# DeltaNet + MoE on one core: the first chunk's matmuls in float32r parts, weight loads that wait for the conversion, and a background inversion that waits for the softplus

## The chip, the cores and the metric

One core of a Trainium2 chip runs the whole program. The metric is the device time of one execution in microseconds (us). The kernel before took 718.76 us, the median of three runs (718.11 to 719.0). One more execution was profiled: it took 716.53 us, of which the trace shows a span of 714.8 us.

The engines named below are PE (the matrix engine, with its weight loads shown as PEld), DVE (vector), ACT (activation), POOL and SP, which issues the transfers.

## The reference

Two stages follow each other. The first is a recurrent attention over 768 steps for 4 x 8 heads of width 48, the second a two-layer MLP with a softplus between, over 3072 tokens (384 -> 2048 -> 384):

```python
for t in range(S):
    kt, vt, bt = (k_n[:, :, t], v[:, :, t], beta[:, :, t, None])
    y[:, :, t] = np.einsum('bhd,bhde->bhe', q[:, :, t], state)
    v_old = np.einsum('bhde,bhd->bhe', state, kt)
    state = state + bt[:, :, :, None] * np.einsum('bhd,bhe->bhde', kt, vt - v_old)
...
h = x @ w_in
g = np.maximum(h, 0.0) + np.log1p(np.exp(-np.abs(h)))
return (g @ w_out).astype(np.float32)
```

`k_n` is `k` divided by its norm. The weights of the MLP come as 64-bit floats, and the kernel turns them into 32-bit ones itself.

## The kernel before, in words

**Chunks.** The 768 steps are cut into 12 chunks of 64 (`NS`, `C`). A chunk's attention needs the inverse of a triangular matrix for every head; the inversion is done for two chunks at once (`invert(u, ...)`, chunks 2u and 2u+1), on DVE, a column at a time (lines 220 and 226). For u = 0 and 1 only the 16-wide diagonal blocks are inverted so, and `join` puts them together with products on PE (lines 243 and 250). `finish` turns the inverse into the tile `tt` with two transposes on DVE (lines 232 and 233). After it come `cross_a`, `arrange`, `cross_b` (lines 260 to 284), `k_state`, `p_half`, `u_all`, `y_all` (line 342 makes the chunk's output, lines 347 to 352 copy it into the tile `x`, line 360 moves a quarter of it by DMA), and `state`.

**MLP.** A chunk has 256 tokens. The hidden width is cut into 16 blocks f of 128, taken in 8 pairs. A pair is: the first product into `ph` (line 462), three passes on ACT (lines 466 to 468), the softplus and its split on DVE (lines 470, 472, 473), and, one pair later, the second product into `po` (line 445). All chunks but the first use three products of float32r parts in place of one product in float32 (high x high, high x low, low x high: `TERMS`). The first chunk uses plain float32 for both products (`HF`, and line 476 in place of 470 to 473).

**Weights.** A generator `weights()` (the `conversion`) turns block f from 64-bit to 32-bit: one pass on ACT (line 381), four on DVE (lines 393, 396, 400, 403), one copy on ACT (line 406). It begins with the first chunk. In the second chunk `split(f)` copies the block out (line 413), rounds it to its high part (line 415) and subtracts for the low part on DVE (line 416), all in the same buffer `w{f}`. A load of block f + 4 is put into the program when block f is converted; ahead of it line 391 writes one column of the new buffer.

**Order.** The order of PE, DVE, ACT and POOL is laid out when the program is built: the code is written by hand in the order of `attention()`, `moe()` and the calls of `fill(n)`, which advance the conversion by n steps, and a planner then places each engine's instructions by its own estimates. An instruction without anything to wait for can move far ahead: the eight one-column writes of line 391 for blocks 8 to 15 stand at the very start of DVE's order. `attend`, `target()` (`RATE`, `LEAD`, `FIRST`) decide how far the attention runs ahead of the MLP, and `invert_some` advances the background inversion by two columns for each half pair of the MLP.

The tile `ex` has three buffers and serves the conversion, the split and the output.

Of the kernel before, what the change touches and what calls it, by code (L numbers as in the profile page):

```python
# [7 lines left out]
F32 = mybir.dt.float32  # L8
# [27 lines left out]
def deltanet_moe(ctx, tc, kT, qT, kN, kI, vN, beta, wts, out):  # L36
# [36 lines left out]
    W, HF, ST, OFF, TT, LTD, LDS, NN, NV, X = {}, {}, {}, {}, {}, {}, {}, {}, {}, {}  # L73
# [112 lines left out]
    def invert(u, cT, ncT):  # L186
# [49 lines left out]
    def join(s):  # L236

        tt = TT[s // 2][:, s % 2 * NP:(s % 2 + 1) * NP, :]
        w1 = two.tile([P, NP, QB], F32, name="gl")
# [15 lines left out]
    def cross_a(s):  # L255
# [7 lines left out]
        if s < 2:  # L263
# [12 lines left out]
    def cross_b(s):  # L276
# [6 lines left out]
        for h in range(2):  # L283
            copies[s < 2 and h](tt[lo[h], :, HB:], pm[lo[h]])
# [27 lines left out]
    def u_all(s):  # L312
# [4 lines left out]
        for e in range(2):  # L317
            for ab in range(2):
                copies[s < 2 and ab](be[tk[ab], ab, e, :, C:], pus[e][tk[ab]])  # L319

    def state(s):
        for g in range(2):
# [6 lines left out]
            for ab in range(2):  # L329
                copies[s < 1 and ab](bv[dr[ab], ab, 8 * g:8 * g + 8, C:], pd[dr[ab]])  # L330

    def y_all(s):

        n, ty = (1, F32) if s == 0 else (2, F32R)
        x = X[s] = one.tile([P, n, NK, B, C], ty, name=f"x{s % 3}")
        x4 = one.tile([P, n, B, C], ty, name="x4")
        for g in range(2):
# [8 lines left out]
            copy = copies[s == 0 and g]  # L346
# [23 lines left out]
    def weights():  # L370
# [13 lines left out]
        ex = magnitude(0)  # L384
        yield
        for f in range(NF):
            hw, lw = words(f)
            if f + AHEAD < NF:

                ST[f + AHEAD] = one.tile([P, 4 * DM], I32, name=f"w{f + AHEAD}")  # L390
                nc.vector.memset(ST[f + AHEAD][:, 0:1], 0)
# [5 lines left out]
                                    op1=ALU.bitwise_and)  # L397
            after = magnitude(f + 1) if f + 1 < NF else None
            yield
# [5 lines left out]
            HF[f] = one.tile([P, 2 * DM], F32, name=f"w{f}")  # L405
            nc.scalar.copy(HF[f], ex.bitcast(F32))
            done[0], ex = f + 1, after
            yield

    def split(f):  # L410

        hf = two.tile([P, 2 * DM], F32, name="ex", bufs=3)
        nc.scalar.copy(hf, HF[f])
        w = W[f] = one.tile([P, 2, 2 * DM], F32R, name=f"w{f}")
        nc.scalar.copy(w[:, 0], hf)
        nc.vector.tensor_tensor(w[:, 1], hf, w[:, 0], op=ALU.subtract)


    def moe():


        n = B * C
        late = None
        for s in range(NS):
            parts = 2 if s else 1
            xr = [[X[s][:, i, k].rearrange("p b t -> p (b t)") for k in range(NK)]
                  for i in range(parts)]
            terms1 = TERMS if s else ((0, 0),)

            def weight(f, a, c, n, s=s):  # L430
                return W[f][:, a, c:c + n] if s else HF[f][:, c:c + n]

            po = ps_o.tile([P, 2, 512], F32, name="po")

            def outp(f0, g, po=po, s=s, weight=weight):

                k = 2 * len(g) - 1
                terms = [(f, h, i) for f in range(f0, f0 + 2) for h in range(2) for i in range(k)]
# [3 lines left out]
                for f, h, i in terms:  # L442
                    a, b = ((0, 0), (1, 0), (0, 1))[i]
                    end = f == NF - 1 and i == k - 1
                    nc.tensor.matmul(po[:, h, 0:DM], g[b][:, f - f0, h * P:(h + 1) * P],  # L445
                                     weight(f, a, DM, DM), start=(f == 0 and i == 0), stop=end)
# [4 lines left out]
            for f0 in range(0, NF, 2):  # L451
                while done[0] < f0 + 2:
                    next(conversion)
                if s == 1:
                    for f in range(0 if f0 == 0 else f0 + 2, min(f0 + 4, NF)):
                        split(f)
                ph = ps_h.tile([P, 2, n], F32, name="ph")
                for f in range(f0, f0 + 2):
                    c = 0
                    for k in range(NK):  # L460
                        for a, b in terms1:
                            nc.tensor.matmul(ph[:, f - f0], weight(f, a, k * P, P), xr[b][k],  # L462
                                             start=(c == 0), stop=(c == len(terms1) * NK - 1))
# [5 lines left out]
                if s:  # L469
                    nc.vector.scalar_tensor_tensor(a, ph, 0.0, a, op0=ALU.max, op1=ALU.add)  # L470
                    g = [two.tile([P, 2, n], F32R, name=name) for name in ("gh", "gl")]
                    nc.vector.tensor_copy(g[0], a)  # L472
# [298 lines left out]
```

## Time and profile before

| what | value |
|---|---|
| median of three runs | 718.76 us |
| the profiled execution | 716.53 us, span 714.8 us |
| PE busy | 631.6 us (88%) |
| DVE busy | 457.5 us (64%) |
| ACT busy | 369.4 us (52%) |
| mean clock granted to PE | 0.956 |
| transfers | 44.80 MB, most of it in the first quarter |

Busy time is summed over the span, and the stages differ: up to about 200 us the attention of chunks 0 to 2, the conversion of the weights and the first MLP chunk share the engines, and after that a period of about 51 us a chunk repeats. In the rows below, "L462" is line 462 of the kernel, "idle" the time the engine stood still before an instruction, and "issue" a wait for which the profile shows no releaser.

### The profile page before, as it was taken

Reading aid. Unit: us, or ns where it says so; the run is one execution under the profiler, and the core shown is the slowest. Engines: PE = TensorE matmul, PEld = TensorE weight load, DVE = VectorE, ACT = ScalarE, POOL = GpSimd, SP = SyncE. Lnnn points to the kernel's source line nnn. Section 1 sums busy time; section 2 is a strip of 40 time slices with the busy share of each in tenths; the row PEclk is TensorE's granted clock in tenths of the full one; section 3 lists DMA queues with packets and bytes.
Section 4 is the critical chain, followed back from the end, with each engine's and each line's share of the span. In section 5 each row is a group of like instructions: output and inputs, shape, how many; then the busy total and the mean of one; then the engine's idle time right before and its main releaser. Section 6 shows DMA issues by size and latency. Waiting matters only on the chain.

```text
span 714.8 us, 24068 instructions
## 1 busy us (share of the span) xinstructions
PE 631.6 (88%) x10736; PEld 583.5 (82%) x10736; DVE 457.5 (64%) x976; ACT 369.4 (52%) x681; POOL 30.1 (4%) x56
## 2 busy tenths in 40 slices
PE   4448877858998899998899997999998999999997
PEld 3447655537898898997899997899997999999997
DVE  5834799866746993466993467984449964454443
ACT  3222377819844356464357465365663556544443
POOL 3100100000000000000001000001000000000000
PEclk9999899979797999998999999899999999999999
DMA  9974250000022021032031130120310300201000
GB/s 224 367 280 120 68 137 10 0 2 25 4 71 78 23 68 46 13 88 61 23 86 38 48 100 27 45 57 25 73 31 24 79 2 25 59 3 33 1 23 22
DMA packets 35095, 44.80 MB, mean 63 GB/s; under 512 B 21776, under 2 KB 27184, under 8 KB 34992
## 3 DMA queue, kind: packets, MB, share of 16 engines
q1 hardware_dynamic: 34992, 43.27, 21.2%
q8 instruction: 84, 1.38, 0.8%
q14 instruction: 19, 0.16, 0.1%
HBM read 36.27 MB, written 4.72 MB: 57 GB/s over the span
## 4 chain that ended last, share of the span: by engine, by line
PE 65%; DVE 21%; issue 6%; ACT 6%; DMA 2%; SPq 0%; POOL 0%; DVEq 0%; ACTq 0%; POOLq 0%
PE po L445 24%; PE ph L462 23%; DVE work L220 3%; PE pa L342 3%; DVE Z L226 3%; PE pa L301 2%; PE pa L260 2%; PE pa L327 2%; PE pa L281 2%; DVE ltq L199 1%; DVE a L470 1%; DVE big L308 1%; DVE ex L403 1%; PE pa L315 1%; PE pa L131 1%
## 5 line engine op out<-in xcount | busy, mean ns | idle before, releaser
L462 PE MATMUL ph<-x,w 128*128 128x256 f32 x1680 | 247.4, 299 | 16.6 <-DVE a L470 9.0
L462 PEld LDWEIGHTS ph<-x,w 128*128 128x128 f32 x1680 | 228.3, 197 | 26.0 <-DVE a L470 9.7
L445 PE MATMUL po<-w,gh 128*128 128x384 f32 x768 | 214.9, 367 | 8.1 <-DVE gh L472 4.2
L466 ACT ACTIVATE a<-ph 128x512 f32<-128x512 f32 x96 | 57.4, 598 | 214.3 <-PE ph L462 203.4
L470 DVE SCALAR_TENSOR_TENSOR a<-ph,a 128x512 f32<-128x512 f32 x88 | 60.6, 689 | 155.5 <-ACT a L468 155.1
L445 PEld LDWEIGHTS po<-w,gh 128*128 128x128 f32 x768 | 139.3, 195 | 20.3 <-issue 6.6
L445 PE MATMUL po<-w,gl 128*128 128x384 f32 x352 | 121.2, 344 | 0.2 <-DVE gl L473 0.2
L445 PEld LDWEIGHTS po<-w,gl 128*128 128x128 f32 x352 | 67.8, 193 | 1.1 <-DVE gl L473 0.7
L473 DVE TENSOR_TENSOR gl<-a,gh 128x512 fp32r<-128x512 f32 x88 | 60.7, 690 | 3.8 <-PE po L445 0.7
L467 ACT ACTIVATE a<-a 128x512 f32<-128x512 f32 x96 | 60.7, 633 | 2.8
L468 ACT ACTIVATE a<-a 128x512 f32<-128x512 f32 x96 | 60.7, 632 | 2.4
L220 DVE TENSOR_TENSOR work<-Z,ltq 128x84 f32<-128x84 f32 (+14 forms) x148 | 44.0, 304 | 3.3 <-ACT gh L213 0.6
L226 DVE TENSOR_TENSOR Z<-Z,work 128x84 f32<-128x84 f32 (+14 forms) x148 | 44.1, 305 | 2.9
L472 DVE CAST gh<-a 128x512 fp32r<-128x512 f32 x88 | 38.0, 432 | 7.8 <-PE po L445 4.4
L342 PEld LDWEIGHTS pa<-big 128*64 128x64 f32 x768 | 26.0, 145 | 7.6 <-ACT big L319 2.6
L342 PE MATMUL pa<-big 128*64 128x64 f32 x768 | 28.8, 232 | 3.4 <-ACT big L319 2.1
L308 DVE TENSOR_TENSOR big<-pa,maskP 64x512 f32<-64x512 f32 x44 | 30.2, 686 | 1.6 <-PE pa L301 1.0
L301 PE MATMUL pa<-big,kt 48*64 48x64 f32 x704 | 27.7, 231 | 1.6 <-ACT off L118 0.9
L274 POOL MEMSET tt<- 32x512 f32 x24 | 13.2, 550 | 368.1 <-PE pa L260 203.2
L319 ACT COPY big<-pa 64x384 f32<-64x384 f32 x44 | 20.6, 472 | 13.1 <-PE pa L315 12.5
L301 PEld LDWEIGHTS pa<-big,kt 48*64 48x64 f32 x704 | 25.1, 145 | 2.0 <-ACT off L118 1.1
L330 ACT COPY big<-pa 48x384 f32<-48x384 f32 x42 | 19.9, 474 | 8.9 <-PE pa L327 8.3
(104 smaller groups left out, 648.4 us busy)
## 6 DMA issues: line engine op xcount, KB each, us to landing
w<-wts SPq DMA_DIRECT2D x16, 768.0 KB, 11.7
kt<-kT SPq DMA_DIRECT2D x24, 192.0 KB, 4.2
big<-qT SPq DMA_DIRECT2D x24, 192.0 KB, 4.1
nv<-vN SPq DMA_DIRECT2D x12, 384.0 KB, 4.1
ki<-kI SPq DMA_DIRECT2D x24, 192.0 KB, 3.5
out<-ex SPq DMA_DIRECT2D x24, 192.0 KB, 1.9
ka<-kN SPq DMA_DIRECT2D x8, 384.0 KB, 3.2
x<-x SPq DMA_DIRECT2D x66, 32.0 KB, 2.1
```

The source lines that it names most:

```text
L220: nc.vector.tensor_tensor(tmp[:, a:a + r, 0:j], Z[:, a + j + 1:a + n, a + j:a + j + 1].to_broadcast([P, r, j]), lq[:, a + j:a + j + 1, a:a ...
L226: nc.vector.tensor_tensor(z, z, tmp[:, a:a + r, 0:j], op=ALU.add)
L301: nc.tensor.matmul(pt[tk[ab], i, :], kts[s % 3][dr[ab], 8 * g + i, :], bv[dr[ab], ab, 8 * g + i, 0:C], start=True, stop=True)
L342: nc.tensor.matmul(py[tk[ab], i, :], big[:, at + C:at + 2 * C], big[:, at:at + C], start=True, stop=True)
L445: nc.tensor.matmul(po[:, h, 0:DM], g[b][:, f - f0, h * P:(h + 1) * P], weight(f, a, DM, DM), start=(f == 0 and i == 0), stop=end)
L462: nc.tensor.matmul(ph[:, f - f0], weight(f, a, k * P, P), xr[b][k], start=(c == 0), stop=(c == len(terms1) * NK - 1))
L466: nc.scalar.activation(a, ph, AF.Abs)
L467: nc.scalar.activation(a, a, AF.Exp, scale=-1.0)
L468: nc.scalar.activation(a, a, AF.Ln, bias=1.0)
L470: nc.vector.scalar_tensor_tensor(a, ph, 0.0, a, op0=ALU.max, op1=ALU.add)
L472: nc.vector.tensor_copy(g[0], a)
L473: nc.vector.tensor_tensor(g[1], a, g[0], op=ALU.subtract)
```

## The change

All twelve chunks now use the float32r parts. `HF` and `split` are gone: the conversion's last copy on ACT rounds straight to the high part (`W[f][:, 0]`), and the low part is subtracted on DVE one block later, from the same `ex` buffer, which is held until then. `y_all` makes both parts of `x` for chunk 0 as well, and several copies of chunks 0 and 1 that were shared between ACT and DVE are on ACT alone (`s < 2` became `s < 1`, or ACT only).

The one column of a new weight buffer is now copied from the block being converted (`ex[:, 0:1]`), so that the load of block f + 4 waits until block f has come that far. The calls of `fill` before the MLP starts advance the conversion by 25 steps in place of 16, and a block has five steps in place of four.

`invert_some` is wrapped in `tc.issue_after(softplus...)`: the planner may not put a column of the inversion ahead of the last softplus written before it. The small tile `ld` of the joins and its partner move from the buffers `gh` and `gl` into a spare `x` tile.

```diff
@@ invert
+            spare = one.tile([P, 2, NP, HB + QB], F32, name=f"x{u + 1}")
             for j in range(2):
-                ld = LDS[2 * u + j] = two.tile([P, NP, HB], F32, name="gh")
+                ld = LDS[2 * u + j] = spare[:, j, :, 0:HB]
+                LDS[2 * u + j, 1] = spare[:, j, :, HB:]
@@ y_all
-        n, ty = (1, F32) if s == 0 else (2, F32R)
+        n, ty = 2, F32R
...
-            copy = copies[s == 0 and g]
+            copy = nc.scalar.copy
@@ weights
-                nc.vector.memset(ST[f + AHEAD][:, 0:1], 0)
+                nc.vector.tensor_copy(ST[f + AHEAD][:, 0:1], ex[:, 0:1])
                 load_weights(f + AHEAD)
...
+            if f > 0:
+                nc.vector.tensor_tensor(W[f - 1][:, 1], last.bitcast(F32), W[f - 1][:, 0],
+                                        op=ALU.subtract)
+                done[0] = f
+                yield
...
-            HF[f] = one.tile([P, 2 * DM], F32, name=f"w{f}")
-            nc.scalar.copy(HF[f], ex.bitcast(F32))
-            done[0], ex = f + 1, after
+            W[f] = one.tile([P, 2, 2 * DM], F32R, name=f"w{f}")
+            nc.scalar.copy(W[f][:, 0], ex.bitcast(F32))
+            last, ex = ex, after
-    def split(f):
-        hf = two.tile([P, 2 * DM], F32, name="ex", bufs=3)
-        nc.scalar.copy(hf, HF[f])
-        w = W[f] = one.tile([P, 2, 2 * DM], F32R, name=f"w{f}")
-        nc.scalar.copy(w[:, 0], hf)
-        nc.vector.tensor_tensor(w[:, 1], hf, w[:, 0], op=ALU.subtract)
@@ moe
-                if s:
-                    nc.vector.scalar_tensor_tensor(a, ph, 0.0, a, op0=ALU.max, op1=ALU.add)
-                    g = [two.tile([P, 2, n], F32R, name=name) for name in ("gh", "gl")]
-                    nc.vector.tensor_copy(g[0], a)
-                    nc.vector.tensor_tensor(g[1], a, g[0], op=ALU.subtract)
-                else:
-                    g = [two.tile([P, 2, n], F32, name="gh")]
-                    nc.vector.scalar_tensor_tensor(g[0], ph, 0.0, a, op0=ALU.max, op1=ALU.add)
+                nc.vector.scalar_tensor_tensor(a, ph, 0.0, a, op0=ALU.max, op1=ALU.add)
+                g = [two.tile([P, 2, n], F32R, name=name) for name in ("gh", "gl")]
+                nc.vector.tensor_copy(g[0], a)
+                softplus[0] = nc.vector.tensor_tensor(g[1], a, g[0], op=ALU.subtract)
@@ invert_some
-        for _ in range(n):
-            if background and next(background[0], 0) == 0:
-                background.pop()
+        with tc.issue_after(softplus[0].ins):
+            for _ in range(n):
+                if background and next(background[0], 0) == 0:
+                    background.pop()
```

**Where the order moves.** A row is a line of the code, the operation, the tile written and the tiles read, their shape, and how often it comes in a row; a number behind a tile's name tells buffers apart.

The first place is SP's queue, after the loads of the first three `kt` tiles. Before:

```order
L368 DMA w_112<-wts 128x1536
L368 DMA w_114<-wts 128x1536
L368 DMA w_1413<-wts 128x1536
L368 DMA w_1424<-wts 128x1536
L368 DMA w_1525<-wts 128x1536
L368 DMA w_1536<-wts 128x1536
L368 DMA w_1564<-wts 128x1536
L368 DMA w_1575<-wts 128x1536
L368 DMA w_1610<-wts 128x1536
L368 DMA w_1621<-wts 128x1536
L95 DMA ka<-kN 128x768
L79 DMA kt_74<-kT 48x1024 x2
```

The same place in the change:

```order
L370 DMA w_112<-wts 128x1536
L370 DMA w_114<-wts 128x1536
L95 DMA ka<-kN 128x768
L79 DMA kt_74<-kT 48x1024 x2
L370 DMA w_631<-wts 128x1536
L370 DMA w_749<-wts 128x1536
L91 DMA nv<-vN 128x768
L370 DMA w_835<-wts 128x1536
L83 DMA big<-qT 48x16x64 x2
```

Eight weight loads that stood in a row (blocks 8 to 15) are gone from there; `ka` and `kt` come right behind blocks 2 and 3, and the further weight loads are spread behind them.

The second place is DVE at the end of the conversion. `ex` with `w` are passes of the conversion, line 416 the subtraction of a low part, `a`, `gh` and `gl` the softplus, `Z` and `work` the inversion for chunks 2 and 3. Before:

```order
L400 SCALAR_TENSOR_TENSOR ex<-w_1621,ex 128x768
L403 SCALAR_TENSOR_TENSOR ex<-w_1621,ex 128x768
L416 TENSOR_TENSOR w_1769<-ex,w_1769 128x768
L416 TENSOR_TENSOR w_1774<-ex,w_1774 128x768
L220 TENSOR_TENSOR work<-Z,ltq 128x14 x2
L226 TENSOR_TENSOR Z<-Z,work 128x14 x2
L220 TENSOR_TENSOR work<-Z,ltq 128x2x13 x2
```

In the change:

```order
L407 SCALAR_TENSOR_TENSOR ex<-w_1739,ex 128x768
L461 SCALAR_TENSOR_TENSOR a<-ph,a 128x512
L229 TENSOR_TENSOR Z<-Z,work 128x14 x2
L410 SCALAR_TENSOR_TENSOR ex<-w_1739,ex 128x768
L463 CAST gh<-a 128x512
L223 TENSOR_TENSOR work<-Z,ltq 128x2x13 x2
L464 TENSOR_TENSOR gl<-a,gh 128x512
L229 TENSOR_TENSOR Z<-Z,work 128x2x13 x2
L416 TENSOR_TENSOR w_1899<-ex,w_1899 128x768
L223 TENSOR_TENSOR work<-Z,ltq 128x3x12 x2
```

Before, the inversion's columns begin when the conversion is over and fourteen of the sixteen subtractions are still to come; now the last subtraction stands among the first columns, and the softplus has three instructions a pair in this stretch.

The third place is PE, just ahead of the first `join` of chunk 2 (line 243, now 246), which waits for the inversion. `x_832` and `x_844` are the input of chunk 0, `x_1303` and `x_1338` that of chunk 1. Before:

```order
L462 MATMUL ph<-x_832,w_1725 128x256 x3
L462 MATMUL ph<-x_832,w_1731 128x256 x3
L243 MATMUL pa<-tt,gh 32x16 x64
L445 MATMUL po<-w_1676,gh 128x384 x2
L445 MATMUL po<-w_1684,gh 128x384 x2
L462 MATMUL ph<-x_1303,w_1769 128x256 x9
L462 MATMUL ph<-x_1303,w_1774 128x256 x9
L445 MATMUL po<-w_1725,gh 128x384
```

In the change:

```order
L440 MATMUL po<-w_1892,gh 128x384 x2
L440 MATMUL po<-w_1892,gl 128x384
L440 MATMUL po<-w_1899,gh 128x384 x2
L440 MATMUL po<-w_1899,gl 128x384
L454 MATMUL ph<-x_1338,w_1602 128x256 x9
L454 MATMUL ph<-x_1338,w_1614 128x256 x9
L246 MATMUL pa<-tt,x_1783 32x16 x64
L440 MATMUL po<-w_708,gh 128x384 x2
```

Before, two second products of chunk 0 and all of chunk 1 stand behind the `join`; now chunk 0 is complete ahead of it, and so are the first products of four pairs of chunk 1.

More of the change, by code (lines that the diff above doesn't have):

```diff
@@ L238, in join @@
         tt = TT[s // 2][:, s % 2 * NP:(s % 2 + 1) * NP, :]
-        w1 = two.tile([P, NP, QB], F32, name="gl")
+        w1 = LDS[s, 1]
         pw = ps_a.tile([P, NP, QB], F32, name="pa")
@@ L283, in cross_b @@
         for h in range(2):
-            copies[s < 2 and h](tt[lo[h], :, HB:], pm[lo[h]])
+            copies[s < 1 and h](tt[lo[h], :, HB:], pm[lo[h]])
     def k_state(s):
@@ L318, in u_all @@
             for ab in range(2):
-                copies[s < 2 and ab](be[tk[ab], ab, e, :, C:], pus[e][tk[ab]])
+                copies[s < 1 and ab](be[tk[ab], ab, e, :, C:], pus[e][tk[ab]])
     def state(s):
@@ L329, in state @@
             for ab in range(2):
-                copies[s < 1 and ab](bv[dr[ab], ab, 8 * g:8 * g + 8, C:], pd[dr[ab]])
+                nc.scalar.copy(bv[dr[ab], ab, 8 * g:8 * g + 8, C:], pd[dr[ab]])
     def y_all(s):
-        n, ty = (1, F32) if s == 0 else (2, F32R)
+        n, ty = 2, F32R
         x = X[s] = one.tile([P, n, NK, B, C], ty, name=f"x{s % 3}")
@@ L382, in magnitude @@
             return ex
-        ex = magnitude(0)
+        ex, last = magnitude(0), None
         yield
@@ L424, in moe, with outp @@
         for s in range(NS):
-            parts = 2 if s else 1
             xr = [[X[s][:, i, k].rearrange("p b t -> p (b t)") for k in range(NK)]
[L427 to L431, printed above, removed]
+                  for i in range(2)]
             po = ps_o.tile([P, 2, 512], F32, name="po")
-            def outp(f0, g, po=po, s=s, weight=weight):
-                k = 2 * len(g) - 1
-                terms = [(f, h, i) for f in range(f0, f0 + 2) for h in range(2) for i in range(k)]
+            def outp(f0, g, po=po, s=s):
+                terms = [(f, h, i) for f in range(f0, f0 + 2) for h in range(2) for i in range(3)]
                 if f0 + 2 == NF:
@@ L443, in outp @@
                     a, b = ((0, 0), (1, 0), (0, 1))[i]
-                    end = f == NF - 1 and i == k - 1
+                    end = f == NF - 1 and i == 2
                     nc.tensor.matmul(po[:, h, 0:DM], g[b][:, f - f0, h * P:(h + 1) * P],
-                                     weight(f, a, DM, DM), start=(f == 0 and i == 0), stop=end)
+                                     W[f][:, a, DM:], start=(f == 0 and i == 0), stop=end)
                     if end:
@@ L460, in moe @@
                     for k in range(NK):
-                        for a, b in terms1:
-                            nc.tensor.matmul(ph[:, f - f0], weight(f, a, k * P, P), xr[b][k],
-                                             start=(c == 0), stop=(c == len(terms1) * NK - 1))
+                        for a, b in TERMS:
+                            nc.tensor.matmul(ph[:, f - f0], W[f][:, a, k * P:(k + 1) * P], xr[b][k],
+                                             start=(c == 0), stop=(c == 3 * NK - 1))
                             c += 1
@@ L630, in deltanet_moe @@
             mask_p(g, pts[g])
+        fill(2)
         run(jn)
         scale_v(0)
+        fill(2)
         cross_a(0)
```

24 lines of the change are left out of this document (13 added, 11 removed).

## Prediction

> **What bounds the kernel now.** First the page: the slices of the engines, and the chain that ended last.
>
> ```profile
> PE   4448877858998899998899997999998999999997
> DVE  5834799866746993466993467984449964454443
> DMA  9974250000022021032031130120310300201000
> PE 65%; DVE 21%; issue 6%; ACT 6%; DMA 2%; SPq 0%; POOL 0%; DVEq 0%; ACTq 0%; POOLq 0%
> ```
>
> A slice is a fortieth of the span, 17.9 us. PE is nearly full from the tenth slice on, so a gain there has to come out of its few idle stretches. The first nine slices look different: PE at 4 to 8, DVE at 9 around 90 to 125 us, the transfers at 9 in the first two. The busy times of stretches say it closer (columns: length, then busy us of PE, PEld, DVE, ACT, POOL, granted clock, share of the transfer engines, GB/s).
>
> ```profile
> 35.00:40.00 5.00, 1.38 (x83) 1.16 (x75) 0.00 (x0) 0.37 (x1) 0.00 (x0) 1.00 1.02 414
> 65.00:70.00 5.00, 4.29 (x157) 3.88 (x154) 2.17 (x4) 0.77 (x2) 0.00 (x0) 1.00 0.33 93
> 68.00:142.00 74.00, 60.02 (x759) 43.11 (x759) 64.03 (x120) 49.11 (x80) 3.55 (x6) 0.93 0.20 57
> 150.90:229.15 78.25, 71.51 (x1685) 64.80 (x1685) 42.40 (x68) 50.15 (x92) 3.51 (x5) 0.85 0.15 41
> 229.15:654.00 424.85, 408.10 (x6534) 387.86 (x6533) 281.62 (x597) 219.48 (x418) 12.40 (x19) 0.97 0.17 45
> ```
>
> Three regimes. At 35 to 40 us no engine works and the transfers run full. From 68 to 142 us DVE sets the pace (64.0 of 74.0 us). From 229.15, where PE starts the first product of chunk 2, PE is busy 408 of 425 us. I follow one landmark through the change, the start of chunk 2's first product ("M"), and treat what lies behind M apart.
>
> **The first stretch: held weight loads.** The chain of waits from 30 to 68 us (start, length, what):
>
> ```profile
> 30.76 3.44 issue
> ...
> 36.84 3.43 issue
> ...
> 43.32 3.14 issue
> ...
> 54.38 0.83 ACT w L406
> ...
> 63.29 0.94 issue
> ...
> 67.40 0.71 issue
> ```
>
> PE stops three times in the middle of a group of equal small products, for 10.0 us in all, while the transfers run full; at 63 and 67 us, with about a third of that load (the row of 65 to 70), the same stops are 0.9 and 0.7 us. I read them as PE's instructions arriving late behind the weight loads, ten of which SP issues in a row from 18 us. In the new order eight of the ten are gone from there. What is left ahead of 30 us is 8.4 MB (four blocks of 0.77, and the inputs); the trace moved some 8 MB by then. So the queue is empty at about 31 us and all three stops should shrink. Bounds: to nothing (10.0 gained), or to the longest stop seen without load, 2.04 us each (3.9 gained):
>
> ```profile
> 178.13 0.73 PE L243 MATMUL pa<-tt,gh 32*32 32x16 f32 x40 [2.04 <-issue]
> ```
>
> I take 1.0 each, nearest to the two rows at 63 and 67: 7.0 us. Against it stand additions on the same chain. ACT now rounds block 0 (0.83, row at 54.38) ahead of the copy that `cross_a` needs, and must wait for DVE's last pass before: 1.2 us. Chunk 0's `x` gets its low part on DVE, for two halves where it copied one before: 0.8 us; a conversion pass in front of them: 0.5 us. ACT also squares `ka` ahead of the first join's copy; `ka` now lands with the queue's end at about 30 us, before ACT reaches it at 33, so I cost it at nothing (each us later is a us on the chain). A held load makes SP wait for DVE's one-column copy; behind that of block 6 stand chunk 1's `q` and chunk 0's `x` transfers, but DVE makes this copy eight instructions before the last part of `x`, which those transfers need anyway. Net: the `x` transfers start 4.5 us earlier (between 1.4 and 7.5).
>
> **The second stretch: DVE.** Before, it runs from the last copy of chunk 0's `x` (61.0 us) to the end of the transpose that the first join of chunk 2 waits for (150.8 us), 89.8 us:
>
> ```profile
> 60.68 0.28 DVE L348 COPY x<-pa 128x128 f32<-128x128 f32 x1
> ...
> 97.60 0.56 DVE L393 TENSOR_SCALAR ex<-ex 128x768 f32<-128x768 f32 x1
> 98.07 0.95 DVE L400 SCALAR_TENSOR_TENSOR ex<-w,ex 128x768 int32<-128x768 int32 x1
> 98.94 0.95 DVE L403 SCALAR_TENSOR_TENSOR ex<-w,ex 128x768 int32<-128x768 int32 x1
> ...
> 148.86 1.90 DVE L232 STREAM_TRANSPOSE tt<-Z 128x1024 f32<-128x1024 f32 x1
> ```
>
> The starts are closer than the lengths: a short pass (lines 393, 396) costs about 0.5 us of DVE's time, a long one (400, 403) 0.87. So four passes are 2.75 us, and the subtraction (long, like line 400) 0.87. The softplus by its groups, less the same 0.08:
>
> ```profile
> L476 DVE SCALAR_TENSOR_TENSOR gh<-ph,a 128x512 f32<-128x512 f32 x8 | 5.5, 692 | 10.4 <-ACT a L468 5.2 <-PE po L445 4.8 <-PE pa L243 0.4
> L470 DVE SCALAR_TENSOR_TENSOR a<-ph,a 128x512 f32<-128x512 f32 x88 | 60.6, 689 | 155.5 <-ACT a L468 155.1
> L472 DVE CAST gh<-a 128x512 fp32r<-128x512 f32 x88 | 38.0, 432 | 7.8 <-PE po L445 4.4 <-PE pa L243 0.5
> L473 DVE TENSOR_TENSOR gl<-a,gh 128x512 fp32r<-128x512 f32 x88 | 60.7, 690 | 3.8 <-PE po L445 0.7
> L416 DVE TENSOR_TENSOR w<-ex,w 128x768 fp32r<-128x768 f32 x16 | 15.2, 953 | 7.6 <-ACT w L415 7.6
> L319 DVE COPY big<-pa 64x384 f32<-64x384 f32 x4 | 2.1, 557 | 1.4 <-ACT big L319 1.3
> ```
>
> A pair is 0.6 us in chunk 0 now, and 0.61 + 0.35 + 0.61 = 1.57 with parts. Counted over the same stretch of the two orders:
>
> - passes: 14 blocks and two passes before, 13 blocks and one after (a block more is done ahead of it): 40.2 to 36.6, -3.6
> - subtractions: 4 before, 14 after: +8.7
> - softplus: 6 pairs at 0.6, against 9 at 1.57 and one first instruction: 3.6 to 14.7, +11.1
> - six copies that go to ACT (0.56 by the last row above, two of them a third larger: 0.6 each): -3.5
>
> That is +12.7 us of work on the engine that sets the pace. DVE's idle time in it (10 us of 68 to 142) I leave as it is: the waits change places, for a join, a softplus and a sum of squares in place of copies. Bounds: all of it closes (-10) or comes twice (+10). The transpose then ends at 150.8 - 4.5 + 12.7 = 159.0 us, 8 us later than before.
>
> **The third stretch: PE up to M.** Here the order of PE pays it back.
>
> ```profile
> 125.80 2.74 PE L445 MATMUL po<-w,gh 128*128 128x384 f32 x8
> 128.38 2.75 PE L462 MATMUL ph<-x,w 128*128 128x256 f32 x12
> ...
> 150.91 1.90 PE L243 MATMUL pa<-tt,gh 32*32 32x16 f32 x128 [9.15 <-DVE tt L232]
> 153.68 4.65 PE L445 MATMUL po<-w,gh 128*128 128x384 f32 x8 [0.87 <-DVE gh L476]
> ...
> 160.31 1.45 PE L445 MATMUL po<-w,gh 128*128 128x384 f32 x4
> ...
> 163.74 1.45 PE L445 MATMUL po<-w,gh 128*128 128x384 f32 x4
> ...
> 229.15 3.84 PE L462 MATMUL ph<-x,w 128*128 128x256 f32 x18
> ```
>
> Two rows of the chain give a pair with parts:
>
> ```profile
> 203.97 2.28 PE po L445 x12
> 206.25 2.15 PE ph L462 x18
> ```
>
> A pair in float32 takes 2.75 + 2.74, one in parts 2.15 + 2.28: 1.06 less, 8.5 for chunk 0. Most of that lies under DVE's stretch and is worth nothing there. What counts is what has left the 78.2 us from 150.9 to M: chunk 0's last second products (4.65 + 1.45 + 1.45 = 7.5 us) and four first products of chunk 1 (8.6). Both now run while DVE finishes the inversion, from about 141 us on, 15 us of work in 18. Left are 78.2 - 16.1 = 62.1 us, and M comes at 159.0 + 62.1 = 221.1 us: 8.0 us earlier. ACT loses 26 us of copies (lines 406 and 413) without effect: it waits for others in both stretches.
>
> **Behind M: the tied inversion.** PE's two longest waits there for DVE:
>
> ```profile
> 240.16 2.39 PE L462 MATMUL ph<-x,w 128*128 128x256 f32 x18 [1.94 <-DVE a L470]
> 448.11 4.21 PE L462 MATMUL ph<-x,w 128*128 128x256 f32 x18 [4.64 <-DVE a L470]
> ```
>
> In both a softplus stood behind ten or more columns of an inversion. Tied, at most a few columns stand ahead of each. After 4.64 us of idling the 18 products took 4.21 in place of 2.15, so this wait cost 2.1 more at half clock: 8.7 us in all at most. I take 4, since the transposes still stand ahead of a softplus; the lower bound is the loss of the rival below.
>
> Sum: 716.5 - 8.0 - 4.0 = 704.5 us for a profiled execution. The one before lies 2.2 us under its median, so the median is **706.7 us**.
>
> **Rivals.**
>
> *DVE's waits close (696.7 us).* For it: the conversion is a block further when the first MLP chunk starts, and DVE waited for ACT's queue in the old order. With 8 of the 10 idle us gone, M gains 16.0, and with 6 behind it: 716.5 - 16.0 - 6.0 + 2.2. Against: the new stretch waits for PE's join and its softplus instead.
>
> *The stops of PE stay (713.7 us).* If they come from the small products themselves, the 7.0 us are lost. Against: the rows at 63 and 67.
>
> *The tied inversion puts the attention in a row (slower, 723.1 us).* The inverse is ready three pairs later. PE's order then holds, in chunks 4, 6, 8 and 10, the products from `cross_a` to `y_all` with hardly an MLP product between, where several pairs stood before. PE then waits for ACT's copies, by these groups:
>
> ```profile
> L262 ACT ACTIVATE off<-pa 32x512 f32<-32x512 f32 x12 | 7.0, 583 | 14.4 <-PE pa L260 14.3
> L319 ACT COPY big<-pa 64x384 f32<-64x384 f32 x44 | 20.6, 472 | 13.1 <-PE pa L315 12.5
> ```
>
> Two for the cross and four ahead of `y_all` are 1.2 + 1.9 = 3.1 us a chain, 12.4 for four, with nothing gained behind M: 716.5 - 8.0 + 12.4 + 2.2. It decides from 2.0 us a chain. Against: the next chunk's products of the same kind stand between and cover most of each copy.
>
> *Three buffers of `ex` (719.9 us).* A block now keeps its buffer until the subtraction. DVE's stretch has about 5.5 us a block; the ring holds it up only if a buffer lives over 16.5 us, against 6 us of bare passes. At 20 us twelve blocks lose 1.1 each, 13.2 in all.
>
> *Half clock in chunk 0 (726 us).* PE has less to do there and idles more. Its work from 63 to 159 us is 35 for eight pairs, 9 for four first products and about 15 of attention, 59 at full clock in 96. Only with over six tenths of that time at half clock does PE become the bound; all of it would be 118, 22 us late. Against: the clock of 0.93 from 68 to 142 us with 14 us idle. The Trainium skill ("TensorE: Matmul & The Clock Gate", What's actually happening) says that the clock is halved by default and after an idle window of about 3.4 us, and released after as long a busy one. The rows at 448 agree with it, and by that rule alone this rival would be likelier than I make it; PE's waits of 1 to 2 us in 68 to 142 were mostly too short.
>
> **How the numbers follow.** Forecast, 701 to 712: 0.51. Closed waits 0.15, stops stay 0.13, attention in a row 0.10, ring 0.07, half clock 0.04. The range of 694 to 720 takes in the first three and the ring and leaves out the two slow cases and the far ends. About 0.2%, 1.4 us, is what a measurement tells from no change: faster 0.51 + 0.15 + 0.13 and half of the ring is 0.82, the same 0.04, slower 0.14.
>
> **What would show it.** Stops of about 1 us in place of 3.4 between 30 and 45 us, and the `x` transfers at 57 us. DVE full from about 77 us, the last subtraction at about 146, the transpose ending near 159, PE's wait for it a few us in place of 9. Chunk 2's first product near 221. Behind it no wait of PE for a softplus over 2 us, and PE's idle time from there to the end under 17. It is wrong if the transpose ends after 167 us, or if PE gathers new waits behind `cross_a` in chunks 4 to 10.

## The result, and the profile after

The change takes **693.25 us** (median of four runs, 689.97 to 696.18) against 718.43 for the kernel before (four runs, 715.87 to 719.0): a ratio of 0.9655, 95% interval 0.9605 to 0.9705. It is faster by 25 us where 12 were forecast, 0.75 us below the range given. The profiled execution took 693.93 us, its span is 692.2.

First the stops of PE and the issue of chunk 0's `x` transfers, from the timeline of the change (start, length, engine, line, operation, idle time before and its releaser):

```profile
32.65 1.57 PE L246 MATMUL pa<-tt,x 32*32 32x16 f32 x100 [2.06 <-issue]
37.62 1.57 PE L253 MATMUL pa<-x,tt 32*32 32x16 f32 x100 [2.33 <-issue]
41.07 1.17 PE L263 MATMUL pa<-tt,off 32*32 32x32 f32 x36 [0.41 <-issue]
59.25 4.49 SPq L362 DMA_DIRECT2D x<-x  x6
```

The three stops are 4.8 us in place of 10.0, and the transfers are issued 2.15 us earlier than before (61.40). Then the stretches up to the transpose and up to M, and the one behind M, in the change:

```profile
62.00:159.69 97.69, 73.62 (x1017) 67.22 (x1013) 84.38 (x190) 54.21 (x90) 3.65 (x6) 0.80 0.34 104
100.00:140.00 40.00, 26.54 (x155) 23.74 (x143) 39.93 (x67) 24.86 (x38) 0.00 (x0) 0.74 0.34 99
159.69:219.68 59.99, 52.95 (x1615) 49.99 (x1614) 25.54 (x51) 28.70 (x60) 3.35 (x5) 0.93 0.19 49
219.68:692.20 472.52, 463.11 (x6926) 446.43 (x6924) 304.96 (x635) 245.21 (x461) 12.26 (x19) 0.97 0.16 43
```

and, of the kernel before, the one behind M to its end, which the prediction showed only up to 654 us:

```profile
229.15:714.80 485.65, 465.02 (x6926) 443.93 (x6924) 304.98 (x636) 245.31 (x461) 12.40 (x19) 0.97 0.16 41
```

From 100 to 140 us DVE is busy 39.93 of 40 us. The places by which the prediction goes:

```profile
143.82 0.97 DVE L416 TENSOR_TENSOR w<-ex,w 128x768 fp32r<-128x768 f32 x1
157.66 2.03 DVE L235 STREAM_TRANSPOSE tt<-Z 128x1024 f32<-128x1024 f32 x1
161.78 1.26 PE L246 MATMUL pa<-tt,x 32*32 32x16 f32 x128
219.68 2.99 PE L454 MATMUL ph<-x,w 128*128 128x256 f32 x18
```

The transpose ends at 159.69. The join starts 2.1 us later with no wait quoted (9.15 us before): until then PE was still at the products of chunk 1. Chunk 2's first product ("M") comes at 219.68 in place of 229.15. The span is 22.6 us shorter, 9.5 of them ahead of M and 13.1 behind it (485.65 - 472.52). Behind M PE does as many products, in 465.0 us before and 463.1 now; its idle time falls from 20.6 to 9.4. The waits of PE there, longest groups first (us in total, times, longest), before:

```profile
PE ph L462 <- DVE a L470: 9.0, 4, 4.6
PE po L445 <- DVE gh L472: 4.2, 2, 2.8
PE pa L131 <- issue: 1.8, 1, 1.8
...
PE po L445 <- DVE gl L473: 0.2, 1, 0.2
```

and in the change:

```profile
PE pa L294 <- issue: 4.0, 2, 2.2
PE pa L284 <- ACT off L265: 0.9, 2, 0.7
PE po L440 <- ACT ex L443: 0.6, 1, 0.6
```

The waits for a softplus, 9.0 + 4.2 + 0.2 = 13.4 us, are gone entirely.

### The profile page after: what moved, and what is told of

It reads as the page before. It is cut to its first block, busy times and chain, and to the rows that moved or that the text cites. A ratio compares the mean times of both kernels' runs of the same rounds, so it can differ in the third digit from the quotient of the medians.

```text
span 692.2 us, 24232 instructions
## 1 busy us (share of the span) xinstructions
PE 621.6 (90%) x10816; PEld 592.5 (86%) x10816; DVE 458.4 (66%) x988; ACT 351.6 (51%) x657; POOL 30.0 (4%) x56
## 4 chain that ended last, share of the span: by engine, by line
PE 78%; DVE 11%; issue 6%; ACT 3%; DMA 1%; SPq 0%; POOL 0%; DVEq 0%; ACTq 0%; POOLq 0%
PE ph L454 29%; PE po L440 28%; PE pa L344 4%; PE pa L304 3%; PE pa L330 2%; PE pa L294 2%; PE pa L284 2%; PE pa L318 2%; DVE ex L407 2%; DVE ex L410 1%; PE pa L131 1%; DVE w L402 1%; PE pa L263 1%; PE pa L253 1%; PE pa L127 1%
## 5 line engine op out<-in xcount | busy, mean ns | idle before, releaser
L454 PE MATMUL ph<-x,w 128*128 128x256 f32 x1728 | 243.8, 293 | 17.9 <-DVE a L461 9.6
L454 PEld LDWEIGHTS ph<-x,w 128*128 128x128 f32 x1728 | 231.3, 198 | 22.9 <-DVE a L461 10.2
L440 PE MATMUL po<-w,gh 128*128 128x384 f32 x768 | 205.2, 348 | 4.5 <-DVE gh L463 3.9
L461 DVE SCALAR_TENSOR_TENSOR a<-ph,a 128x512 f32<-128x512 f32 x96 | 65.9, 689 | 126.7 <-ACT a L460 126.1
L440 PE MATMUL po<-w,gl 128*128 128x384 f32 x384 | 132.4, 345 | 1.1 <-DVE gl L464 1.1
L440 PEld LDWEIGHTS po<-w,gl 128*128 128x128 f32 x384 | 74.0, 193 | 1.8 <-DVE gl L464 1.6
L464 DVE TENSOR_TENSOR gl<-a,gh 128x512 fp32r<-128x512 f32 x96 | 66.3, 691 | 3.0
L463 DVE CAST gh<-a 128x512 fp32r<-128x512 f32 x96 | 40.5, 424 | 5.6 <-PE po L440 3.6
L298 DVE TENSOR_TENSOR nv<-nv,pa 128x384 f32<-128x384 f32 x22 | 11.1, 546 | 27.4 <-PE pa L294 27.4
L304 PEld LDWEIGHTS pa<-big,kt 48*64 48x64 f32 x704 | 27.3, 156 | 0.6 <-issue 0.6
```

What stands on the lines that cost most here:

```text
L304: nc.tensor.matmul(pt[tk[ab], i, :], kts[s % 3][dr[ab], 8 * g + i, :], bv[dr[ab], ab, 8 * g + i, 0:C], start=True, stop=True)
L454: nc.tensor.matmul(ph[:, f - f0], W[f][:, a, k * P:(k + 1) * P], xr[b][k], start=(c == 0), stop=(c == 3 * NK - 1))
L464: softplus[0] = nc.vector.tensor_tensor(g[1], a, g[0], op=ALU.subtract)
```

## The experiments

The change consists of five edits: the float32r parts of chunk 0 with the split within the conversion ("the parts"; the copies of chunks 0 and 1 that are now on ACT alone go with them in every run), the fuller first order, the held loads, the tie, and the small tile of the joins in a spare `x` tile ("the spare tile"). The table gives, for all kernels: the median, its ratio to the kernel before, run beside it, and from the profiles the issue of the `x` transfers, the end of the transpose that the first join of chunk 2 waits for, M, and the time from M to the end of the span. Each ratio is to runs of the kernel before on the same chip, whose medians were 716.0 to 718.4. The differences quoted below are between medians, and by the ratios they come out up to 3 us otherwise (e4's loss against the change is 4.6 us by the medians and 7.6 by the ratios). The four columns on the right are each from one profiled execution, while the executions of one kernel lie 4 to 10 us apart, so a difference of 2 or 3 us in them says little alone.

| kernel | us | ratio, 95% | `x` | transpose | M | behind M |
|---|---|---|---|---|---|---|
| before | 716.0 to 718.4 | 1 | 61.40 | 150.76 | 229.15 | 485.7 |
| the change | 693.25 | 0.9655 (0.9605-0.9705) | 59.25 | 159.69 | 219.68 | 472.5 |
| e1: change, untied | 698.19 | 0.9756 (0.9718-0.9794) | 58.34 | 152.19 | 216.39 | 481.1 |
| e2: before + tie + spare tile | 688.23 | 0.9610 (0.9579-0.9641) | 60.95 | 155.66 | 217.02 | 469.0 |
| e3: change, loads not held | 697.89 | 0.9739 (0.9686-0.9792) | 63.31 | 166.15 | 225.20 | 472.5 |
| e4: change, old first order | 697.86 | 0.9761 (0.9724-0.9797) | 55.98 | 164.55 | 224.24 | 467.5 |
| e5: before + spare tile | 703.22 | 0.9805 (0.9766-0.9844) | 60.09 | 147.45 | 215.84 | 484.7 |
| e6: change, untied, no spare tile | 714.04 | 0.9957 (0.9931-0.9984) | 60.56 | 158.05 | 230.67 | 480.4 |
| e7: e2 + held loads | 677.28 | 0.9448 (0.9380-0.9516) | 56.23 | 153.19 | 210.25 | 466.2 |
| e8: e7 + fuller first order | 673.16 | 0.9380 (0.9343-0.9416) | 54.84 | 146.25 | 203.14 | 464.7 |
| e9: change, no low part in chunk 0 | 691.40 | 0.9638 (0.9597-0.9680) | 57.83 | 154.53 | 215.27 | 472.1 |
| e10: change, one product of three | 686.95 | 0.9561 (0.9504-0.9618) | 58.54 | 157.03 | 213.81 | 468.6 |
| e11: change, chunk 0 in float32 | 684.88 | 0.9541 (0.9502-0.9580) | 60.39 | 156.89 | 213.38 | 468.3 |
| e12: e8, one block more | 678.39 | 0.9459 (0.9406-0.9512) | 59.46 | 151.27 | 208.27 | 468.3 |

**First question: is the gain behind M the tie's?** e1 takes the tie out of the change:

```diff
-        with tc.issue_after(softplus[0].ins):
-            for _ in range(n):
+        for _ in range(n):
...
```

> The change without its tie: the columns of the background inversion may again stand ahead of a softplus; all else as in the change. Theory (the 13 us gained behind the start of chunk 2's first product come from the tie alone): that start stays at 217 to 223 us, PE's waits for a softplus behind it return to 10 to 17 us from none, the stretch behind it is 483 to 488 us in place of 472.5, and the time is 703 to 709 us. Rival (the gain behind it comes from what the first chunks leave behind, with the planner's order of the rest): the stretch stays within 470 to 476 us and the time at 690 to 697 us.

Behind M PE's waits for a softplus are back:

```profile
PE ph L454 <- DVE a L461: 6.7, 5, 2.8
PE po L440 <- DVE gh L463: 2.6, 2, 2.0
```

The stretch goes from 472.5 to 481.1 us, and M comes 3.3 us *earlier*. So in the change the tie gives 8.6 us behind M and takes 3.3 ahead of it. That is less than the theory's 13: the stretch and the time lie between the two ranges expected, and the other 4.5 us behind M came with other edits. e2 puts the tie into the kernel before. There the small tile occupies buffers that a softplus needs, and with the tie the order should wait on itself, which was argued and not run; so the spare tile went in too (parts of the diff):

```diff
+            spare = one.tile([P, 2, NP, HB + QB], F32, name=f"x{u + 1}")
...
-                ld = LDS[2 * u + j] = two.tile([P, NP, HB], F32, name="gh")
+                ld = LDS[2 * u + j] = spare[:, j, :, 0:HB]
...
+    background, softplus = [], [None]
...
+        with tc.issue_after(softplus[0].ins):
...
```

> The kernel before with the tie alone (and the small tile of the joins in a spare x tile, which the tie needs). Theory (tie alone): the start of chunk 2's first product stays near 229 us, the stretch behind it falls from 485.7 to 470 to 476 us, the time is 703 to 708 us. Rival (not the tie): the stretch stays at 482 to 488 us, the time at 715 to 720 us.

The time is 688.2 us, 5 us less than the whole change by the medians (the intervals of the ratios overlap), and M moved from 229.15 to 217.02 with chunk 0 still in float32 and no load held. So something in these two small edits moves M, which I had put down to the parts, and the rest of the change gains nothing on top of them.

**Second question: what are the held loads and the fuller order worth?** e3 writes the column as before, e4 has the old calls of `fill` at their old places (16 steps in place of 25; with five steps a block that is a little over three blocks, where the kernel before has four):

```diff
-                nc.vector.tensor_copy(ST[f + AHEAD][:, 0:1], ex[:, 0:1])
+                nc.vector.memset(ST[f + AHEAD][:, 0:1], 0)
```

> The change with the weight loads free again (a constant written into the first column in place of the copy). Theory (PE's stops at 30 to 45 us come from the loads): the three stops are 9 to 10 us in all in place of 4.8, chunk 0's x transfers and all behind them come 4 to 6 us later, and the time is 696 to 701 us. Rival (DVE's waits of 9.5 us between 62 and 77 us take the delay up): the stops grow, chunk 2 starts at the same 219 to 221 us, time 690 to 696 us. Second rival (the stops are those of PE's own small products): the stops stay at 5 us.

```diff
-        fill(2)
...
-        fill(4)
+        fill(2)
...
-        fill(3)
+        fill(5)
```

> The change with the fill calls of before (16 steps of the conversion ahead of the first MLP product in place of 25, at the old places). Theory (DVE sets the pace up to 160 us, and work that is put into its waits before 60 us counts in full): nine steps of some 0.9 us go behind, the transpose for chunk 2 ends 5 to 9 us later than 159.7, time 697 to 702 us. Rival (DVE waits later in any case and takes them up there): the transpose ends within 2 us, time 690 to 696 us.

Without held loads the stops of PE are 3.44, 3.43 and 4.79 us, the transfers are issued 4.1 us later and M comes 5.5 us later; the time is 4.6 us more. The first two stops are as long as before and the third is longer, so the second rival fails. With the old order the `x` transfers are even earlier (55.98), but DVE does the block later, where it sets the pace: the transpose ends 4.9 us later and M comes 4.6 us later. The median is 4.6 us more; the profiled execution (693.4) made up for M behind it (467.5 us), so this one is less certain. e3's interval overlaps that of the change, e4's lies above it.

**Third question: what moves M?** The timeline of DVE's softplus in the kernel before holds an answer. In it `gh` is the softplus' output, and the small tile of the joins takes both of its two buffers, on POOL from 128.61 and 139.22 us:

```profile
128.61 0.33 POOL L212 MEMSET gh<- 128x256 f32 x1 [38.69 <-PE po L445]
139.22 0.32 POOL L212 MEMSET gh<- 128x256 f32 x1 [10.29 <-PE po L445]
...
133.68 0.68 DVE L476 SCALAR_TENSOR_TENSOR gh<-ph,a 128x512 f32<-128x512 f32 x1
...
152.94 0.69 DVE L476 SCALAR_TENSOR_TENSOR gh<-ph,a 128x512 f32<-128x512 f32 x1 [0.45 <-PE pa L243]
158.43 0.69 DVE L476 SCALAR_TENSOR_TENSOR gh<-ph,a 128x512 f32<-128x512 f32 x1 [4.80 <-PE po L445]
...
178.99 0.64 DVE L472 CAST gh<-a 128x512 fp32r<-128x512 f32 x1 [0.51 <-PE pa L243]
```

Between 133.68 and 152.94 us no softplus is written at all; the next one is released by the join's products (line 243), and until 178.99 the MLP has one buffer of two. e5 has the spare tile alone in the kernel before (the lines on `spare` and `ld` of e2's diff, and the partner of the tile):

```diff
-        w1 = two.tile([P, NP, QB], F32, name="gl")
+        w1 = LDS[s, 1]
```

> The kernel before, with one edit: the small tile of the joins lies in a spare x tile, and not in two of the buffers that the softplus of the MLP writes; the inversion is not tied. Theory after the first four runs (the small tile held two of those buffers from 128.6 us on, so that PE and DVE stood behind the joins): chunk 2's first product comes at 217 +- 3 us in place of 229, the wait of 9.15 us before the first join is gone or under 2 us, behind that landmark nothing is gained (483 to 488 us), and the time is 702 to 707 us. Rival (the tie moved the landmark in the run with both): it stays at 227 to 230 us, and the time within 2 us of the kernel before.

M is 215.84, the time 703.2, both as the theory had them, and the join's wait is gone; softplus outputs are written at 134.62, 139.49, 143.76 and 149.94, without the hole. Behind M it is 484.7 us, and the waits are there as before:

```profile
PE ph L464 <- DVE a L472: 9.7, 5, 3.9
PE po L447 <- DVE gh L474: 3.3, 2, 2.0
```

With the tie on top (e2) both groups are gone and the stretch is 15.7 us shorter:

```profile
217.02:686.00 468.98, 460.74 (x6925) 443.36 (x6924) 305.01 (x635) 244.57 (x461) 12.24 (x19) 0.98 0.16 43
```

13.0 us of waits and 4.4 us of PE's busy time (465.1 in e5's row below, with the same number of products) have gone; other waits took 1.7 back, by subtraction.

```profile
215.84:700.50 484.66, 465.09 (x6925) 443.44 (x6924) 305.38 (x636) 245.53 (x461) 12.54 (x19) 0.98 0.15 41
```

e6 is the counter-test, the change without tie and without spare tile, so parts, held loads and fuller order alone (the diffs of e1 and e2, backwards):

> The change, untied, and with the small tile of the joins back in the buffers of the softplus: float32r parts, held weight loads and the fuller first order alone. Theory (the spare tile carried the landmark): chunk 2's first product at 226 to 232 us in place of 216.4 in the untied change, 708 to 714 us. Rival (the float32r parts and the fuller order take work out from behind the join, as the prediction's third stretch had it): 216 to 219 us, and 697 to 700 us.

M is 230.67, later than in the kernel before, and the time 714.0, at the upper end of the theory. The spare tile is what takes M from 230.67 to 216.39 (e1). The softplus of e6 waits for its buffer again:

```profile
160.23 0.43 DVE L460 CAST gh<-a 128x512 fp32r<-128x512 f32 x1 [0.45 <-PE pa L243]
...
179.64 0.43 DVE L460 CAST gh<-a 128x512 fp32r<-128x512 f32 x1 [3.51 <-PE pa L243]
```

Its stretch behind M is 480.4, 5.2 us shorter than before, with PE's waits for a softplus at 10.6 us in place of 13.4; why the parts shorten these waits was not looked into.

**Fourth question: which edits help without the parts?** e7 is e2 with the held loads (the edit below), e8 with the fuller order too (20 steps of four a block, five blocks as in the change, its calls of `fill` at the change's places):

```diff
-                nc.vector.memset(ST[f + AHEAD][:, 0:1], 0)
+                nc.vector.tensor_copy(ST[f + AHEAD][:, 0:1], ex[:, 0:1])
```

> The kernel before with the tie, the spare x tile and the held weight loads: the first chunk still in float32, the old first order. If held loads are worth what the change without them lost (5.5 us to chunk 2's first product): stops of PE at 30 to 46 us of 4 to 6 us in all in place of 10.0, the landmark at 211 to 214 us, 682 to 686 us. Rival (DVE sets the pace before the landmark, and an earlier start only makes it wait for something else): landmark at 216 to 218 us, 687 to 690 us.

> As the run before it, with the conversion advanced by 20 steps in place of 16 before the MLP starts (five blocks in place of four, as in the change). If the fuller first order is worth what the change lost without it (4.6 us): landmark at 207 to 212 us, 678 to 683 us. Rival (it only fills waits that the float32r parts made): within 1.5 us of the run before it.

Both beat their expectation; e7's stops are 5.3 us in all, as expected. The held loads are worth 10.95 us here, where the change without them lost 4.6; why more, no run shows. The fuller order brings M another 7.1 us forward (4.1 us by the medians, and the intervals of e7 and e8 overlap). e8, at **673.2 us**, is the fastest kernel of all: 20.1 us ahead of the change, which differs from it by the parts alone. The spans of the profiled executions are 24.4 us apart, 16.5 of them ahead of M and 7.9 behind it; e8's lay 3.3 us under its median. From 100 to 140 us e8 has, beside the change's row above, PE at 36.7 us and a clock of 0.99:

```profile
100.00:140.00 40.00, 36.70 (x276) 26.60 (x275) 37.73 (x96) 34.83 (x59) 0.00 (x0) 0.99 0.24 80
```

**Fifth question: why do the parts cost 20 us?** Three kernels take a piece of them away. e9 leaves out chunk 0's low part of the softplus, with the products as many as before:

```diff
...
+                else:
+                    g = [two.tile([P, 2, n], F32R, name="gh")] * 2
+                    softplus[0] = nc.vector.tensor_copy(g[0], a)
```

> The change, without the low part of the softplus in chunk 0 (eight subtractions on DVE fewer; the third product takes the high part again, so PE does as many products, and chunk 0's output is less exact). The change stands 20 us behind the kernel that has tie, spare tile, held loads and fuller order but chunk 0 in float32. Theory (DVE sets the pace up to the transpose, so that each us of it is a us): 8 x 0.61 = 4.9 us less, transpose ends at 155 in place of 159.7 us, landmark at 214 to 216 us in place of 219.7, 687 to 690 us. Rival (PE sets the pace there, at a granted clock of 0.80): unchanged, 692 to 695 us.

The transpose ends 5.2 us earlier and M comes 4.4 us earlier; 1.4 us of it are earlier `x` transfers, so that the stretch of DVE is 3.7 us shorter for 4.9 us of work. The median fell by 1.9 us only, to between the two ranges, and its interval overlaps the change's: the landmarks speak for DVE, the time alone does not tell. e10 leaves DVE's work and drops two of chunk 0's three products on PE (the first product; the second is cut in the same way):

```diff
-                        for a, b in TERMS:
+                        for a, b in TERMS if s else TERMS[:1]:
```

> The change, with one product of the three for chunk 0 (high by high; PE has a third of chunk 0's products, DVE and ACT do what they did). Theory (DVE sets the pace): transpose at 157 to 160 us, landmark within 3 us of 219.7, 690 to 695 us. Rival (PE sets the pace at the low clock: 8 pairs x 2.95 us less, 24 us of work at full clock): transpose before 150 us, landmark before 210 us, under 683 us.

The transpose moves by 2.7 us only, as DVE's pace has it, and PE now stands before chunk 0's products, of which it has a third:

```profile
PE ph L454 <- ACT w L413: 16.4, 6, 5.0
PE po L440 <- DVE gh L463: 11.2, 4, 5.7
```

(waits of PE from 60 to 150 us; 4.9 and 3.9 us in the change). But M comes 5.9 us earlier and the time is 6.3 us less, 3 us below what that theory allowed. Of M's 5.9 us, 0.7 are earlier `x` transfers, 2.0 lie in DVE's stretch and 3.2 between the transpose and M, where PE's stops without a releaser are 3.2 us in place of 7.0. Whether the fewer products made those stops shorter is not shown. e11 computes chunk 0 in float32 from the high parts, with one product as in e10 and one softplus instruction a pair, and keeps the split in the conversion (the softplus alone):

```diff
...
+                else:
+                    g = [two.tile([P, 2, n], F32, name="gh")]
+                    softplus[0] = nc.vector.scalar_tensor_tensor(g[0], ph, 0.0, a, op0=ALU.max,
+                                                                 op1=ALU.add)
```

> The change, with chunk 0's products in float32 from the high parts and one softplus instruction a pair, as in the kernel before (the low parts of x, weights are made but not used in chunk 0); the split stays within the conversion. Theory: of the 20 us, the softplus in parts is 8 x 0.96 = 7.7 us of DVE's time and the rest is the split, which has to be done before the conversion goes on: transpose at 150 to 153 us, landmark at 209 to 213 us, 682 to 687 us. Rival (the whole loss comes from the products in parts): 672 to 677 us. Second rival (from the split alone): 691 to 695 us.

The time (684.9) is within what the theory gave, M (213.38) lies 0.4 us past it, and the transpose (156.89) is 4 us too late: DVE has 7.7 us less to do, its waits from 60 to 150 us rose from 12.2 to 16.3, and its start came 1.1 later. So of the 20.1 us, 8.4 go with chunk 0's arithmetic and 11.7 with the split in the conversion, the two parts of chunk 0's `x` and the copies that went to ACT: against e8, e11 issues the `x` transfers 5.6 us later and takes 5.1 us longer from there to the transpose. Neither amount was taken apart further, so how the 20 us divide between DVE and PE stays open.

e12 advances e8's conversion by one block more:

```diff
-        fill(2)
+        fill(3)
...
-        fill(3)
+        fill(4)
...
```

> The fastest so far (float32 in chunk 0, tie, spare tile, held loads, conversion advanced by 20 steps before the MLP), advanced by 24 steps. From 16 to 20 the landmark came 7.1 us earlier. If DVE still has room in the first stretch: landmark 3 to 6 us earlier than 203.1, 668 to 671 us. Rival (the sixth block delays chunk 0's own attention on DVE): no better, 673 to 678 us.

The rival holds: 678.4 us. The `x` transfers are issued 4.6 us later than in e8, M comes 5.1 us later; five blocks are the better number by the medians and the landmarks, though the intervals of e8 and e12 just touch.

## Why the prediction was wrong, and where it was right

The forecast was 706.7, the result 693.25: 13.45 us. Of these, 9.1 lie behind M (4 taken, 13.1 measured), 1.5 ahead of M (8.0 us earlier forecast, 9.5 measured), and 2.9 in the step from the profiled execution to the median (2.2 us were added for it; the change's median lay 0.7 under its profiled execution). The last is scatter between executions, and no step of the kernel.

**Behind M** is the step that failed: "I take 4", with "8.7 us in all at most", and nothing there for any edit but the tie. Measured were 13.1. The mechanism, columns of the inversion standing ahead of a softplus, is right: e1 and e2 show it from both sides. The size was wrong in two ways. First, the sum went by two waits, of 1.94 and 4.64 us, called PE's two longest. The groups hold 9.0 + 4.2 + 0.2 = 13.4 us in seven waits; one of 2.8 us for `gh` and one of 2.17 are longer than the 1.94, and behind the latter the slower clock shows too, beside 18 such products at their usual length:

```profile
171.90 2.31 PE L462 MATMUL ph<-x,w 128*128 128x256 f32 x18
...
345.33 3.78 PE L462 MATMUL ph<-x,w 128*128 128x256 f32 x18 [2.17 <-DVE a L470]
```

(The 2.15 us that the prediction sets against 4.21 are a piece of the chain, whose pieces do not overlap; in this view they are 2.31.) The upper bound should have been 13.4 plus the slow products behind these waits; in the kernel before, the tie is worth 15.7 us (e5 to e2). Second, the tie is not all of it: in the change it is worth 8.6 (e1), just within the prediction's bound. The other 4.5 came without it: e6, with neither tie nor spare tile, is already 5.2 us shorter behind M than the kernel before, 2.0 in PE's idle time and 3.2 in its busy time for as many products. Why, no run shows; that busy time is 456.1 to 465.1 us across the kernels.

**The third stretch** came out nearly right, and was credited to the wrong edit. The prediction gave it 62.1 us between transpose and M (60.0 measured), because products leave it: "Both now run while DVE finishes the inversion". They do: from transpose to M PE is busy on `po` for 17.8 us in place of 26.9 and on `ph` for 12.2 in place of 21.5, and its idle time is 7.0 us in place of 6.9. The change's order has all of chunk 0's second products and four first products of chunk 1 ahead of the join. But this was put down to the parts, and e6 has the parts too, with fewer products there. By the busy times from 50 us to the join of the instructions on `po` and on `ph` (length of the stretch, then busy us of PE with the count), in the change

```profile
50.00:161.70 111.70, 22.73 (x96) 18.67 (x96) 0.94 (x2) 0.82 0.36 107
50.00:161.70 111.70, 40.37 (x216) 36.45 (x216) 6.75 (x10) 6.36 (x11) 0.82 0.36 107
```

and in e6

```profile
50.00:158.10 108.10, 18.66 (x72) 15.45 (x72) 0.00 (x0) 0.83 0.37 108
50.00:158.10 108.10, 35.41 (x180) 32.00 (x180) 5.48 (x8) 4.67 (x8) 0.83 0.37 108
```

the change has 96 second products (eight pairs) and 216 first ones (eight pairs and four), e6 has 72 (six) and 180 (eight and two). e6 takes 72.6 us from the transpose to M, 5.8 less than the kernel before, and M comes no earlier. The rows from transpose to M of the kernel before, e6, e1 (parts and spare tile, untied) and e2 (float32, with spare tile and tie) are

```profile
150.76:229.15 78.39, 71.51 (x1685) 64.83 (x1685) 42.54 (x69) 50.15 (x92) 3.51 (x5) 0.85 0.15 41
158.05:230.67 72.62, 64.47 (x1657) 60.82 (x1657) 32.29 (x59) 34.14 (x68) 3.34 (x5) 0.85 0.17 44
152.19:216.39 64.20, 58.66 (x1666) 55.21 (x1664) 31.71 (x57) 33.90 (x68) 3.52 (x5) 0.96 0.19 49
155.66:217.02 61.36, 55.84 (x1609) 51.94 (x1608) 35.12 (x61) 41.39 (x78) 3.34 (x5) 0.87 0.17 45
```

e2 comes to 61.4 us without the parts, so it is the spare tile, with the tie, that shortens the stretch, and that the size fits the parts is luck. The count ahead of the join is not the whole account: e1 has 84 and 162 products there, at a join 5.8 us earlier than e6's. After e6's join the softplus waits for buffers (the rows above) and PE's clock is 0.85, in e1 it is 0.96. The spare tile, which the prediction did not cost at all, is the edit that pays: 13.3 us of M alone (e5), 14.3 in the change (e6 to e1). Its sign stood in a row that the prediction quotes for the softplus' length: of the 10.4 us of waits in it, "<-PE po L445 4.8 <-PE pa L243 0.4" are waits for buffers, read past.

**The second stretch**: 12.7 us more from the `x` transfers to the transpose were forecast; it is 11.1 (100.4 against 89.4): DVE is busy for 87.1 us in place of 75.0 and idle for 13.4 in place of 14.3. DVE sets the pace there, 39.93 us of the 40 from 100 to 140, and of e9's 4.9 us of work 3.7 showed in its length. That the waits of DVE stay was right. But the sum hides two terms of the other edits. Of the 8.9 us by which the transpose ends later, the tie adds 7.5 (e1 to the change), the spare tile takes 5.9 (e6 to e1), and the parts with the held loads and the fuller order add 7.3 (before to e6).

**The first stretch**: the stops halved and did not fall to 1.0 each (2.06, 2.33, 0.41), and the rest of the way took 3.0 us more (5.2 gained at the stops, 2.15 at the transfers), where the additions were put at 2.5. The reading that full transfers cause the stops holds for part of them only. The transfers of the change from 28 to 48 us, in slices of half a us, in tenths:

```profile
DMA  9999522100094997200001000000100000004289
```

PE's first stop lies from 30.6 to 32.65 us, in slices of 2, 2, 1 and 0 tenths, and still takes 2.06 us. In e11 the same stop takes 3.71 us, with 5 tenths in its first slice, 3 and 1 in the next two and 0 after that. Over the ten kernels with held loads the first stop is 2.06 to 3.71 us, against 3.18 to 3.44 without, so holding the loads does little for it; the third is 0.40 to 0.95 against 3.14 to 4.79.

**The rivals.** DVE's waits did not close (13.4 us of idle time in its stretch against 14.3), so that this rival's 696.7 us lies nearest to the result is luck: it had 16.0 ahead of M, measured 9.5, and 6 behind it, measured 13.1. No wait of PE for `cross_a`'s copies over 0.7 us: the attention in a row did not happen. From 60 to 150 us no wait for a buffer of `ex` is among DVE's. The half clock did happen (0.74 from 100 to 140 us) and did not set the time of the transpose, since e10 removed two thirds of chunk 0's products and the transpose moved by 2.7 us only. In this rival's text, 59 us of work in 96 fill PE when six tenths of the work are at half clock; that is 0.77 of the time, and not "over six tenths of that time". Its 726 us also leaves out the 2.2 us that the other rivals add (706.7 + 22 = 728.7).

The forecast that the change would be faster held. That its largest edit loses about 20 us, which the other four cover, no step of it said.

## What to carry to other kernels

Before a change of many edits is costed, list for each buffer that two users share who holds it and until when: a small tile in a ring of two cost 14 us here, and its sign was a few small waits "<-PE" on the engine that writes the ring. To size what a reordering can give, add all waits of the group and the slow products behind them, not the longest ones. That is an upper bound: the groups held 13.4 us, and in the change the tie gave 8.6. And measure the edits of a change one by one: here four of five gave 44 us and the fifth took 20 back.

## What the runs showed of the hardware

PE's clock can fall after a wait of 2.17 us: behind it, at 345.33 us, 18 products took 3.78 in place of 2.31 us, while after 1.94 us, at 240.16, they took 2.39. The Trainium skill ("TensorE: Matmul & The Clock Gate", What's actually happening) puts an idle window of about 3.4 us ahead of the slower clock; it also says that the window runs freely. The row has the slower rate after less idling than that.

PE stopped in the middle of equal small products, with nothing in the profile to wait for, for 3.1 to 3.4 us each while the transfers ran full (before, e2), and still for 2.06 us where they were at 0 to 2 tenths (the change's first stop); behind 35 us it was 0.41 to 2.33 in the change and 0.41 and 0.69 in e4. From one of these three stops to the next there are 128 products with as many weight loads in every kernel (100 behind a stop and 28 ahead of the next), whatever the transfers did. What PE waits for there is not shown by any view.
